# Down-weight pieces loaded earlier, and early down products moved into batch 0's chain, in an attention and feed-forward kernel

## The chip, the cores and the metric

The kernel runs on one core of one Trainium2 chip. The metric is the device time of the whole program in microseconds; the median of several runs is taken. The kernel before takes 239.7 us.

Five engines matter here: TensorE (PE; its weight loads are listed apart as PEld), VectorE (DVE), ScalarE (ACT), GpSimd (POOL), which in this kernel also issues nearly all loads, and SyncE (SP), which issues the stores.

## The reference

Eight batches, eight heads, 576 tokens, head size 64, 32 memory slots. Attention runs through the memory slots, and its output feeds a bilinear feed-forward layer with d_model 512 and d_ff 1536:

```python
a = exp(phi - max) ; a = a / sum(a)             # over the 576 tokens
k_m = einsum('bhsm,bhsd->bhmd', a, k)           # 32 slots per head
v_m = einsum('bhsm,bhsd->bhmd', a, v)
attn = softmax(q @ k_m.T / 8)                   # [576, 32] per head
x = (attn @ v_m) as [4608 tokens, 512]
out = ((x @ w_a) * (x @ w_b)) @ w_out           # f32 out
```

The kernel folds v_m into w_a and w_b, so that x itself is never formed: with A the normalised attention (256 rows, heads x slots), x @ w_a is A times (v_m @ w_a).

## The kernel before

The order of instructions on each engine is the order in which the program emits them. The schedule is written by hand as strings of short names, which call "units". The loads, all on one queue issued by GpSimd, at the start:

```python
load_phi(0); load_q(0, halves); load_v(0)          # batch 0's inputs (k comes by SP and ACT)
...
load_wab(0, 256)                                    # w_a and w_b, first third in two parts
load_wab(256, 512)
...
load_wab(512, 1024)                                 # second third
nc.gpsimd.memset(kv_sbs[1][:, 2], 1.0 / CS)
load_wab(1024, 1536)                                # last third
...
for x in "o0 p o1 k q0 q1 o2 o3 v0 v1 o4 o5".split():
    loads[x]()
```

Here o0 to o5 are the six pieces of w_out (two of its twelve row blocks each), p and k are batch 1's phi and k, and q0, q1, v0, v1 are the halves (heads 0 to 3, heads 4 to 7) of batch 1's q and v. The next inputs, batch 2's and 3's, follow in the same queue.

The units of the attention chain of one batch, as the strings name them:

- exp0, exp1: exp of phi (ACT). ks0, ks1: the sums over tokens for k_m of head groups 0 and 1, and the division (PE product pk, DVE kvm). vs0, vs1: the same for v_m.
- qt0 to qt3: transposes of q on DVE (qT); qt0 and qt1 read the half q0, qt2 and qt3 the half q1. kt, vt: transposes of k_m and v_m on PE (pT), copied by DVE (kvT).
- s0, s1: the scores of head group 0 and 1 (PE, pscore). e0, e1: their exp (ACT, E). den: the sums of exp (PE, pD; then the logarithm on ACT, L). nr: exp(-L) on ACT (R), and the product that gives A.
- hv0, hv1 (256 wide), v1, v2 (512 wide): the fold of v_m into a part of w_a (suffix a) or w_b (suffix b) (PE, pva). hx, x: the copies of that fold out of PSUM, one by ACT and one by DVE (vab).
- a3, b3: the up product of row block 3 with w_a or w_b (pa, pb); a1.0 is one half of the tokens. pa is copied by ACT (a_sb, or w_sums as spare room in batch 0), pb is multiplied with it by DVE (ht).
- F2, f8: fills, products of a constant tile into an unused bank, 512 or 128 columns wide.
- y3: three of the early down products. L: the loads of the batch after the next.

The early down products are the first four blocks of output rows:

```python
EARLY = 4
def early_downs():
    pos = [banks.take([P, d_model], F32, "po", hold=True) for c in range(EARLY)]   # four of eight banks
    for n in range(NFF // 2):              # piece n of w_out
        for c in range(EARLY):
            yield from down_part(*pos[c], c, 2 * n, 2 * (n + 1))                   # two products po
```

That is 48 products, eight for each piece of w_out, and four copies of po by ACT (o_sb) at the end. All of them come after batch 0's last up product in the kernel before. Once all are done a "y" does nothing. Later output rows are made by other products (py, pv, px) that combine sums of the weights (w_sums) and sums of ht (h_sums), both made on GpSimd; "d3" pulls three of those, as far as they are ready.

```python
chain(0, "... a3 b0 hv1b hx1b v1a x1a a2 b3 a4 b2 a5 v1b x1b L a7 a6 b5 v2a x2a b6 b7 a8 v2b a11 x2b b4 a9 a10 b10 b8 b9 b11")
chain(1, "y1 exp0 y6 exp1 y3 ks0 y2 qt0 y1 kt0 y2 qt1 ks1 s0 y1 e0 y2 qt2 kt1 y1 den0 qt3 y6 s1 y3 nr0 e1 y1 vs0 vs1 den1 y2 vt0 vt1 nr1 y3 hv0a hx0a hv0b y3 hx0b")
load(3)
sum_weights()
ups(steps(1, 0, 4), slots(1, "d3+y1+hv1a+hx1a hv1b+y3+hx1b - - - y3+v1+x1a+x1b - -"))
ups(half_steps(1, 0, 4), slots(1, "- v2+x2a+x2b+qt0' - - qt1'+exp0' exp1'+qt2' - kv'+km'+y9"))
```

`ups` emits the up products of a batch and, after each step, one slot of the string beside it; a name with ' is the next batch's unit. kv' and km' are batch 2's sums and their division, kvt its transpose.

Of the kernel before, what the change touches and what calls it, by code (L numbers as in the profile page):

```python
# [14 lines left out]
CS = 16.0  # L15
# [3 lines left out]
def kernel(  # L19
# [11 lines left out]
    nc = tc.nc  # L31
# [6 lines left out]
    NFF = d_ff // P  # L38
    NCH = d_ff // 512
# [19 lines left out]
    wa_rows = moe_w_a.rearrange("(c p) f -> p c f", p=P)  # L59
    wb_rows = moe_w_b.rearrange("(c p) f -> p c f", p=P)  # L60
# [4 lines left out]
    wa_sb = wpool.tile([P, NHP, d_ff], F16, name="wa_sb")  # L65
    wb_sb = wpool.tile([P, NHP, d_ff], F16, name="wb_sb")
    wo_sb = wpool.tile([P, NFF, d_model], F16, name="wo_sb")
    w_sbs = (wa_sb, wb_sb)
# [5 lines left out]
    kv_sbs = [consts.tile([P, 3, NHP, NI * D], F16, name=f"kv_sb{t}") for t in range(2)]  # L74

    def load_phi(b):
        phis[b] = inp.tile([P, NHP, NI * M], F32, name="phi_sb")
        nc.gpsimd.dma_start(out=phis[b], in_=rows(phi, b))

    def load_k(b, hps=slice(0, NHP)):  # L80
        kvs[b] = kv_sbs[b % 2]
        nc.gpsimd.dma_start(out=kvs[b][:, 0, hps], in_=rows(k, b)[:, hps])

    def load_v(b, hps=slice(0, NHP)):
        nc.gpsimd.dma_start(out=kvs[b][:, 1, hps], in_=rows(v, b)[:, hps])

    def load_q(b, hps=slice(0, NHP)):
        if b not in qs:
            qs[b] = inp.tile([P, NHP, NI * D], F16, name="q_sb")
        nc.gpsimd.dma_start(out=qs[b][:, hps], in_=rows(q, b)[:, hps])  # L90

    def load(b):
        load_phi(b)
        load_k(b)
        load_v(b)
        load_q(b)

    def load_wab(lo, hi):
        nc.gpsimd.dma_start(out=wa_sb[:, :, lo:hi], in_=wa_rows[:, :, lo:hi])  # L99
        nc.gpsimd.dma_start(out=wb_sb[:, :, lo:hi], in_=wb_rows[:, :, lo:hi])  # L100

    def load_wo(n):
        sl = slice(2 * n, 2 * (n + 1))
        nc.gpsimd.dma_start(out=wo_sb[:, sl, :], in_=wo_rows[:, sl, :])
# [42 lines left out]
    def fill(n, cols=512):  # L147

        pw = banks.tile([P, 512], F32, name="pw")
        for _ in range(n):  # L150
            nc.tensor.matmul(pw[:, :cols], warm[:, :P], warm[:, :cols], start=True, stop=True)
# [4 lines left out]
    for x in halves:  # L156
        nc.vector.tensor_copy(out=kvs[0][:, 0, x], in_=k_f32[:, x])
    load_wab(0, 256)
    load_wab(256, 512)

    ones = consts.tile([P, 4, 32], F16, name="ones")
# [2 lines left out]
                            pattern=[[-32, 4], [0, 32]], channel_multiplier=1)  # L164
    nc.gpsimd.affine_select(out=ones, in_=ones, compare_op=ALU.is_ge, fill=0.0, base=31,
                            pattern=[[32, 4], [0, 32]], channel_multiplier=-1)
    load_wab(512, 1024)
    nc.gpsimd.memset(kv_sbs[1][:, 2], 1.0 / CS)  # L168
    load_wab(1024, 1536)
    loads = {f"o{n}": lambda n=n: load_wo(n) for n in range(NFF // 2)}  # L170
    loads |= {"p": lambda: load_phi(1), "k": lambda: load_k(1)}
    for n, x in enumerate(halves):
        loads[f"q{n}"] = lambda x=x: load_q(1, x)
        loads[f"v{n}"] = lambda x=x: load_v(1, x)
    for x in "o0 p o1 k q0 q1 o2 o3 v0 v1 o4 o5".split():
        loads[x]()

    attn = {}
# [286 lines left out]
    def sum_weights():  # L465
        nc.gpsimd.tensor_copy(out=w_sums[:, 0, 0, 0:1], in_=attn[1][:, 1, S - 1:S])
        t = [w_sums[:, x] for x in range(4)]
        for out, in0, in1 in ((t[0], quarter(0, 1), quarter(0, 0)), (t[1], quarter(1, 1), t[0]),
                              (t[2], quarter(1, 1), quarter(0, 1)), (t[3], quarter(1, 0), t[1])):
            for x in range(2):  # L470
                sl = slice(KH // 2 * x, KH // 2 * (x + 1))
                nc.gpsimd.tensor_tensor(out=out[:, sl], in0=in0[:, sl], in1=in1[:, sl], op=ALU.subtract)
# [157 lines left out]
    def up_half(b, i, hf, x):  # L630
        ps = banks.tile([P, HALF], F32, name=("pa", "pb")[x])
        for g in range(2):
            nc.tensor.matmul(ps, vabs[b][x][:, g, P * i:P * (i + 1)], attn[b][:, g, HALF * hf:HALF * (hf + 1)],  # L633
                             start=(g == 0), stop=(g == 1))
        if x == 0:
            if b == 0:
                n = (2 * i + hf) % 20
                a_sbs[b, i, hf] = spare[:, HALF * n:HALF * (n + 1)]
            else:
                a_sbs[b, i, hf] = apool.tile([P, HALF], F16, name="a_sb")  # L640
            nc.scalar.copy(out=a_sbs[b, i, hf], in_=ps)  # L641
        else:
            t0 = S * (b % 2) + HALF * hf
            nc.vector.tensor_tensor(out=ht[:, i, t0:t0 + HALF], in0=a_sbs.pop((b, i, hf)), in1=ps, op=ALU.mult)  # L644

    def up(b, i, hfs):
        for hf in hfs:
            up_half(b, i, hf, 0)
        if len(hfs) > 1:
            yield  # L650
        for hf in hfs:
            up_half(b, i, hf, 1)
        yield

    def ups(steps, side=()):

        side = iter(side)
        for step in steps:
            for _ in up(*step):
                work.advance()  # L660
                next(side, us[step[0]]["-"])()
        for f in side:
            work.advance()
            f()

    def steps(b, lo, hi):

        return [(b, i, (0, 1)) for i in range(lo, hi)]

    def half_steps(b, hf, lo=0):  # L670

        return [(b, i, (hf,)) for i in range(lo, NFF)]
# [10 lines left out]
    def slots(b, names):  # L683

        def both(fs):
            return lambda: [f() for f in fs]
        def unit(n):
            if n == "fin":
                return lambda: work.pull(-work.done % NFF)
            if n == "L":  # L690
                return lambda: load(b + 2) if b + 2 < B else None
            if n[0] == "y":
                return lambda: some(int(n[1:]))
            if n[0] == "d" and n[1:].isdigit():
                return lambda: work.pull(int(n[1:]))
            return us[b + n.endswith("'") - n.endswith("_")][n.rstrip("'_")]

        return [both([unit(n) for n in x.split("+")]) for x in names.split()]
# [3 lines left out]
    def some(n):  # L702
        for _ in range(n):
            next(early, None)

    def chain(b, plan):


        for x in plan.split():
            if x[0] in "fF":  # L710
                fill(int(x[1:]), P if x[0] == "f" else 512)
            elif x == "L":
                load(b + 2)
            elif x[0] == "y":
                some(int(x[1:]))
            elif x[0] in "ab":
                i, _, hf = x[1:].partition(".")
                for h in ([int(hf)] if hf else (0, 1)):
                    up_half(b, int(i), h, "ab".index(x[0]))
            else:  # L720
                us[b][x]()

    fill(78, P)
    chain(0, "f2 F1 f8 exp0 ks0 F1 exp1 ks1 qt0 qt1 qt2 F2 kt0 F1 kt1 qt3 s0 e0 s1 e1 F2 f2 den00 den10 vs1 nr00 nr10 vs0 den11 den01 vt0 vt1 nr01 f4 hv0a hx0a F1 nr11 f2 hv0b F1 f2 a1.0 hx0b a0.1 hv1a F1 a1.1 hx1a a0.0 b1 a3 b0 hv1b hx1b v1a x1a a2 b3 a4 b2 a5 v1b x1b L a7 a6 b5 v2a x2a b6 b7 a8 v2b a11 x2b b4 a9 a10 b10 b8 b9 b11")
    chain(1, "y1 exp0 y6 exp1 y3 ks0 y2 qt0 y1 kt0 y2 qt1 ks1 s0 y1 e0 y2 qt2 kt1 y1 den0 qt3 y6 s1 y3 nr0 e1 y1 vs0 vs1 den1 y2 vt0 vt1 nr1 y3 hv0a hx0a hv0b y3 hx0b")
    load(3)
    sum_weights()
    ups(steps(1, 0, 4), slots(1, "d3+y1+hv1a+hx1a hv1b+y3+hx1b - - - y3+v1+x1a+x1b - -"))
    ups(half_steps(1, 0, 4), slots(1, "- v2+x2a+x2b+qt0' - - qt1'+exp0' exp1'+qt2' - kv'+km'+y9"))
    work.plan(S + HALF, 10)  # L730
    ups(half_steps(1, 1, 4), slots(2, "- kvt+qt3 - sc+e0+e1 d1 den0+den1+d1+nr0 - v0+nr1+x0a x0b - v1+x1a+x1b -"))
    second = "v2_+d2+x2a_+x2b_+exp0 - exp1 - kv+km+d2 qt0 d4+qt1+kvt qt2 L+d1+qt3+sc+e0 - d2+v0+e1+x0a+x0b - den0+exp0'+d2 v1+nr0+x1a x1b+d10+exp1' - qt0' v2+x2a+x2b+kv' - den1+km0' km1'+kvd' nr1+qt1' qt2' qt3' - d6"
    every = "exp0' sc+exp1'+e0+d3+e1+v0+x0a+x0b+ed - kv'+km0' km1' - d4+sm0 sm1+tn0+kvd' - tn1+d2 d3 v1+qt0'+x1a+ad d3+L+x1b qt1' - qt2' - v2+x2a+x2b - qt3' - - - - -"
    last = "sc e0+e1+ed - v0+x0b - - sm0 x0a+sm1+tn0 d2+v1+d3+x1b+tn1 - ad+d6 x1a - - - - v2+x2a - - - - - x2b"
# [38 lines left out]
```

The softmax here doesn't subtract the row's maximum and nothing guards it: scores larger than these inputs give would overflow.

## Time and profile before

| what | value |
|---|---|
| time, median of 3 | 239.7 us (239.5 to 240.38) |
| span of the profiled run | 238.1 us |
| PE busy | 229.1 us |
| DVE, POOL, ACT busy | 169.0, 155.0, 153.3 us |
| moved by DMA | 37.27 MB, mean 157 GB/s |

Matmuls are pipelined, so a row of the timeline lasts longer than the time until the next product can start; starts, not ends, are used for spacing. What a row waited for stands at its end in brackets, with the idle time just before it. A transfer's landing is its issue plus the time to landing; how busy a queue is stands in the DMA view.

The timeline of the loads' issue on POOL shows that they are not sent all at once: each waits for an earlier transfer to have landed.

```profile
15.86 0.70 POOL L104 DMA_DIRECT2D wo_sb<-in_moe_w_out_dram  x1 [0.59 <-DMA wa_sb<-in_moe_w_a_dram]
...
24.98 0.71 POOL L90 DMA_DIRECT2D q_sb<-in_q_dram  x1 [1.86 <-DMA wb_sb<-in_moe_w_b_dram]
```

The first column is the start in microseconds, the second the length. The first line is o0, the second q1.

### The profile page before, as it was taken

To read this page: it belongs to the slowest core of one execution; us is meant where nothing else is said; L and a number is where in the kernel's file an instruction comes from. 1 tells how busy PE (TensorE), PEld (TensorE's weight loads), DVE (VectorE), ACT (ScalarE), POOL (GpSimd) and SP (SyncE) were. 2 spreads that over 40 slices of the span, in tenths; PEclk is the share of its full clock that TensorE was granted. 3 is DMA by queue.
4 is the path that set the end of the run, shared out by engine and by line. 5 is a ranking of instruction groups with operands and counts; after the bars stand their busy time and mean duration, and the time that the engine had idled before them with its cause. 6 is when DMAs were issued, how large, how long until landed. Compare 5 with 4: busy or idle time off the path is not lost.

```text
span 238.1 us, 7716 instructions
## 1 busy us (share of the span) xinstructions
PE 229.1 (96%) x3064; PEld 168.5 (71%) x3064; DVE 169.0 (71%) x414; ACT 153.3 (64%) x394; POOL 155.0 (65%) x132
## 2 busy tenths in 40 slices
PE   7979898999999999999999999999999999999993
PEld 7735563455756867867787877867787778888882
DVE  4556874468949968979766888689867776756642
ACT  2267751669699488786878458766876777465430
POOL 7953244599979959592979599682929265946001
PEclk9999999999999999999999999999999999999999
DMA  6999999999975999743799648995233342023145
GB/s 232 240 198 206 216 245 207 249 215 278 226 168 140 207 285 224 160 96 77 173 227 207 108 104 184 221 161 132 58 85 68 72 92 49 21 69 71 38 103 148
DMA packets 38436, 37.27 MB, mean 157 GB/s; under 512 B 14688, under 2 KB 32480, under 8 KB 38400
## 3 DMA queue, kind: packets, MB, share of 16 engines
q0 software_dynamic: 19264, 23.14, 52.4%
q1 hardware_dynamic: 18624, 12.85, 24.2%
q10 hardware_dynamic: 512, 0.79, 1.0%
q8 instruction: 24, 0.39, 0.7%
q14 instruction: 12, 0.10, 0.1%
HBM read 42.47 MB, written 9.44 MB: 218 GB/s over the span
## 4 chain that ended last, share of the span: by engine, by line
PE 77%; DMA 12%; POOL 5%; ACT 2%; issue 1%; DVE 1%; DVEq 0%; POOLq 0%
PE py L505 18%; PE pa L633 17%; PE pb L633 17%; PE pv L505 9%; DMA wa_sb<-in_moe_w_a_dram 6%; DMA wo_sb<-in_moe_w_out_dram 6%; PE pva L368 5%; PE px L505 4%; PE po L429 3%; PE pkv L212 2%; PE pscore L297 1%; POOL wb_sb L100 1%; POOL wa_sb L99 1%; POOL kv_sb L168 1%; ACT a_sb L641 1%
## 5 line engine op out<-in xcount | busy, mean ns | idle before, releaser
L644 DVE TENSOR_TENSOR ht<-a_sb,pb 128x288 f16<-128x288 f16 x168 | 71.8, 445 | 33.5 <-ACT a_sb L641 25.6
L633 PEld LDWEIGHTS <-vab 128*128 128x128 f16 x768 | 72.7, 98 | 24.3 <-issue 7.9
L641 ACT CAST a_sb<-pa 128x288 f16<-128x288 f32 x168 | 65.8, 412 | 31.8 <-PE pa L633 28.6
L633 PE MATMUL pa<-A,vab 128*128 128x288 f16 x384 | 75.9, 287 | 0.0
L633 PE MATMUL pb<-A,vab 128*128 128x288 f16 x384 | 75.3, 286 | 0.2
L487 POOL TENSOR_TENSOR h_sums<-ht 128x768 f16<-128x768 f16 x28 | 46.3, 1656 | 25.8 <-DVE ht L644 25.8
L505 PEld LDWEIGHTS <-h_sums 128*128 128x128 f16 x384 | 37.1, 98 | 8.1 <-issue 1.8
L381 ACT CAST vab<-pva 128x512 f16<-128x512 f32 (+1 forms) x60 | 32.0, 583 | 7.3 <-PE pva L368 7.1
L505 PEld LDWEIGHTS <-ht 128*128 128x128 f16 x288 | 27.9, 98 | 5.9 <-issue 0.9
L505 PE MATMUL py<-w_sums,h_sums 128*128 128x256 f16 x192 | 30.5, 273 | 0.0
L381 DVE CAST vab<-pva 128x512 f16<-128x512 f32 (+1 forms) x44 | 26.6, 635 | 4.4 <-PE pva L368 4.4
L487 POOL TENSOR_TENSOR h_sums<-h_sums,ht 128x768 f16<-128x768 f16 x14 | 23.0, 1644 | 1.0
L487 POOL TENSOR_TENSOR h_sums<-ht,h_sums 128x768 f16<-128x768 f16 x14 | 23.0, 1642 | 0.9
L310 ACT ACTIVATE E<-pscore 128x288 f16<-128x288 f32 x32 | 10.8, 419 | 11.8 <-PE pscore L297 11.7
L505 PE MATMUL py<-w_sums,ht 128*128 128x256 f16 x96 | 16.2, 273 | 0.1
L512 ACT ACTIVATE u<-py 128x256 f32<-128x256 f32 x32 | 12.4, 389 | 5.4 <-PE py L505 4.9
L505 PE MATMUL py<-wo_sb,ht 128*128 128x256 f16 x96 | 15.7, 273 | 0.0
L505 PE MATMUL pv<-w_sums,h_sums 128*128 128x256 f16 x96 | 15.7, 273 | 0.0
L505 PE MATMUL px<-wo_sb,ht 128*128 128x256 f16 x96 | 15.2, 273 | 0.0
L203 DVE STREAM_TRANSPOSE qT<-q_sb 128x288 f32<-128x288 f32 x32 | 14.7, 464 | 0.1
L505 PE MATMUL pv<-wo_sb,h_sums 128*128 128x256 f16 x96 | 14.4, 272 | 0.0
L194 ACT ACTIVATE exp_sb<-phi_sb 128x576 f16<-128x576 f32 x16 | 10.9, 697 | 5.0 <-DMA phi_sb<-in_phi_dram 5.0
(70 smaller groups left out, 267.2 us busy)
## 6 DMA issues: line engine op xcount, KB each, us to landing
out_dram<-o_sb SPq DMA_DIRECT2D x68, 128.0 KB, 2.5
phi_sb<-in_phi_dram POOLq DMA_DIRECT2D x8, 576.0 KB, 7.0
kv_sb<-in_v_dram POOLq DMA_DIRECT2D x7, 576.0 KB, 12.1
kv_sb<-in_k_dram POOLq DMA_DIRECT2D x7, 576.0 KB, 9.7
q_sb<-in_q_dram POOLq DMA_DIRECT2D x6, 576.0 KB, 14.4
wo_sb<-in_moe_w_out_dram POOLq DMA_DIRECT2D x6, 256.0 KB, 12.7
q_sb<-in_q_dram POOLq DMA_DIRECT2D x4, 288.0 KB, 10.9
wa_sb<-in_moe_w_a_dram POOLq DMA_DIRECT2D x2, 512.0 KB, 13.9
```

The source lines that it names most:

```text
L194: nc.scalar.activation(out=t["exp"][:, 2 * z:2 * z + 2, :, :], in_=phis[b][:, 2 * z:2 * z + 2, :].rearrange("p c (i m) -> p c i m", m=M), ...
L203: nc.vector.transpose(out=t["qT"][:, hp, :].bitcast(F32), in_=qs[b][:, hp, :].bitcast(F32))
L310: nc.scalar.activation(out=Ev[:, g, :, z, :], in_=pss, func=AF.Exp, scale=1.0 / (8.0 * CS))
L368: nc.tensor.matmul(t["pva", lo, z][g][0][32 * j:32 * j + 32, 0:hi - lo], t["kvT"][64 * r:64 * r + 64, 4 + g, M * j:M * j + M], w_sbs[z][64 ...
L381: engine_copy(out=vabs[b][z][:, g, lo:hi], in_=pva[:, 0:hi - lo])
L429: nc.tensor.matmul(po, ht[:, i, P * c:P * (c + 1)], wo_sb[:, i, :], start=(i == 0), stop=(i == NFF - 1))
L487: engine.tensor_tensor(out=out, in0=in0, in1=in1, op=op)
L505: nc.tensor.matmul(po, lhs[:, i], rhs[:, i], start=first and i == 0, stop=i == KH - 1, skip_group_check=not first)
L512: nc.scalar.mul(out=x, in_=po, mul=scale)
L633: nc.tensor.matmul(ps, vabs[b][x][:, g, P * i:P * (i + 1)], attn[b][:, g, HALF * hf:HALF * (hf + 1)], start=(g == 0), stop=(g == 1))
L641: nc.scalar.copy(out=a_sbs[b, i, hf], in_=ps)
L644: nc.vector.tensor_tensor(out=ht[:, i, t0:t0 + HALF], in0=a_sbs.pop((b, i, hf)), in1=ps, op=ALU.mult)
```

## The change

The pieces of w_out are spread over the load order: the first goes ahead of the last third of the up weights, the others between batch 1's inputs. With that, eight early down products move into batch 0's chain, ahead of and between the folds of the last third, where PE waited for weights; all 48 are done by the end of batch 1's chain. The fills of batch 0's chain and the order of its units are set anew, and so are the slots after it. The aim is that PE has products to do while it would wait for loads.

```diff
-    load_wab(512, 1024)
-    nc.gpsimd.memset(kv_sbs[1][:, 2], 1.0 / CS)
-    load_wab(1024, 1536)
-    loads = {f"o{n}": lambda n=n: load_wo(n) for n in range(NFF // 2)}
+    loads = {"m": lambda: nc.gpsimd.memset(kv_sbs[1][:, 2], 1.0 / CS)}
+    for n in range(1, NCH):
+        for z in range(2):
+            loads[f"w{'ab'[z]}{n}"] = lambda z=z, n=n: load_w(z, 512 * n, 512 * (n + 1))
...
-    for x in "o0 p o1 k q0 q1 o2 o3 v0 v1 o4 o5".split():
+    for x in "m wa1 wb1 o0 wa2 wb2 p o1 k o2 q0 o3 v0 o4 q1 v1 o5".split():
...
-    chain(0, "f2 F1 f8 exp0 ks0 F1 exp1 ks1 qt0 qt1 qt2 F2 kt0 F1 kt1 qt3 s0 e0 s1 e1 F2 f2 den00 den10 vs1 nr00 nr10 vs0 den11 den01 vt0 vt1 nr01 f4 hv0a hx0a F1 nr11 f2 hv0b F1 f2 a1.0 hx0b a0.1 hv1a F1 a1.1 hx1a a0.0 b1 a3 b0 hv1b hx1b v1a x1a a2 b3 a4 b2 a5 v1b x1b L a7 a6 b5 v2a x2a b6 b7 a8 v2b a11 x2b b4 a9 a10 b10 b8 b9 b11")
-    chain(1, "y1 exp0 y6 exp1 y3 ks0 y2 qt0 y1 kt0 y2 qt1 ks1 s0 y1 e0 y2 qt2 kt1 y1 den0 qt3 y6 s1 y3 nr0 e1 y1 vs0 vs1 den1 y2 vt0 vt1 nr1 y3 hv0a hx0a hv0b y3 hx0b")
+    chain(0, "F1 f2 qt0 F1 exp0 F1 ks0 F1 exp1 ks1 qt1 kt0 qt2 F1 f2 F2 kt1 qt3 F1 s0 e0 s1 F1 e1 F1 den10 f2 den00 f2 vs1 nr00 nr10 vs0 den11 den01 vt0 vt1 nr01 hv0a hx0a nr11 hv0b f4 hx0b a0.0 f2 hv1a F1 a0.1 f2 a1.1 hx1a a1.0 b1 a3 hv1b hx1b v1a b0 x1a a2 b3 a4 v1b x1b a5 b5 y3 b2 L a6 y1 v2a x2a y1 b6 y1 a7 y1 a11 v2b x2b y1 b4 a9 b7 a10 a8 b9 b8 b10 b11")
+    chain(1, "y3 exp0 y5 ks0 y1 exp1 qt0 y5 kt0 qt1 ks1 y1 s0 e0 y2 qt2 y1 kt1 y1 den0 y4 qt3 y3 s1 e1 y1 vs0 vs1 nr0 y1 den1 y5 vt0 vt1 nr1 y3 hv0a hx0a hv0b y1 hx0b y3")
...
-    ups(steps(1, 0, 4), slots(1, "d3+y1+hv1a+hx1a hv1b+y3+hx1b - - - y3+v1+x1a+x1b - -"))
-    ups(half_steps(1, 0, 4), slots(1, "- v2+x2a+x2b+qt0' - - qt1'+exp0' exp1'+qt2' - kv'+km'+y9"))
+    ups(steps(1, 0, 4), slots(1, "d5+y1 hv1a+hx1a hv1b+hx1b - - y3+y3+v1+x1a+x1b - -"))
+    ups(half_steps(1, 0, 4), slots(1, "- v2a+v2b+x2a+x2b - qt0'+exp0' - qt1'+y9 exp1' qt2'+kv'+km'"))
...
-    ups(half_steps(1, 1, 4), slots(2, "- kvt+qt3 - sc+e0+e1 d1 den0+den1+d1+nr0 - v0+nr1+x0a x0b - v1+x1a+x1b -"))
+    ups(half_steps(1, 1, 4), slots(2, "- kvt+qt3 - sc+e0+e1 den0+den1+d1+nr0 - - nr1 v0+x0a+x0b - v1a+v1b+x1a+x1b+d5 -"))
```

`load_w` loads a stretch of w_a or of w_b; `load_wab` calls it for both.

More of the change, by code (lines that the diff above doesn't have):

```diff
@@ L96, in load, with load_w @@
         load_q(b)
+    def load_w(z, lo, hi):
+        nc.gpsimd.dma_start(out=w_sbs[z][:, :, lo:hi], in_=(wa_rows, wb_rows)[z][:, :, lo:hi])
     def load_wab(lo, hi):
-        nc.gpsimd.dma_start(out=wa_sb[:, :, lo:hi], in_=wa_rows[:, :, lo:hi])
-        nc.gpsimd.dma_start(out=wb_sb[:, :, lo:hi], in_=wb_rows[:, :, lo:hi])
+        for z in range(2):
+            load_w(z, lo, hi)
     def load_wo(n):
@@ L166 @@
                             pattern=[[32, 4], [0, 32]], channel_multiplier=-1)
-    load_wab(512, 1024)
-    nc.gpsimd.memset(kv_sbs[1][:, 2], 1.0 / CS)
-    load_wab(1024, 1536)
-    loads = {f"o{n}": lambda n=n: load_wo(n) for n in range(NFF // 2)}
+    loads = {"m": lambda: nc.gpsimd.memset(kv_sbs[1][:, 2], 1.0 / CS)}
+    for n in range(1, NCH):
+        for z in range(2):
+            loads[f"w{'ab'[z]}{n}"] = lambda z=z, n=n: load_w(z, 512 * n, 512 * (n + 1))
+    loads |= {f"o{n}": lambda n=n: load_wo(n) for n in range(NFF // 2)}
     loads |= {"p": lambda: load_phi(1), "k": lambda: load_k(1)}
```

## The prediction

> **What bounds the kernel now.** I read the page's busy shares first, then the table of windows, the PE timeline of the first 65 us, the POOL timeline for the transfers, and the DVE and ACT timelines of the stretch that the change rewrites.
>
> The page: TensorE is busy 96% of the span; no other engine passes 71%.
>
> ```profile
> PE 229.1 (96%) x3064; PEld 168.5 (71%) x3064; DVE 169.0 (71%) x414; ACT 153.3 (64%) x394; POOL 155.0 (65%) x132
> ```
>
> The windows (stretch, its length, busy us of PE, PEld, DVE, ACT, POOL, then clock and DMA) say where the other 4% lies: PE has gaps before 49 us and hardly any from 100 us to 220 us. So a rewritten start can only gain what PE loses there, 1.36 + 1.27 + 0.50 us in these three rows.
>
> ```profile
> 8.00:20.00 12.00, 10.64 (x275) 6.10 (x273) 5.92 (x21) 6.47 (x19) 8.27 (x12) 1.00 1.32 202
> 20.00:37.00 17.00, 15.73 (x159) 9.90 (x161) 12.46 (x29) 11.08 (x30) 5.67 (x9) 1.00 1.22 225
> 37.00:49.00 12.00, 11.50 (x248) 5.05 (x235) 5.58 (x18) 5.24 (x14) 6.74 (x11) 1.00 1.20 230
> ...
> 140.00:180.00 40.00, 39.96 (x514) 30.33 (x513) 30.80 (x76) 29.02 (x75) 27.59 (x20) 1.00 0.76 139
> ```
>
> The PE timeline (start, length, engine, line, operation, tiles, count, idle before) names the four waits on transfers that the change is aimed at, and two rows I use as anchors:
>
> ```profile
> 27.25 0.41 PE L368 MATMUL pva<-wa_sb,kvT 64*32 64x512 f16 x8 [0.20 <-DMA wa_sb<-in_moe_w_a_dram]
> ...
> 29.80 0.41 PE L368 MATMUL pva<-wb_sb,kvT 64*32 64x512 f16 x8 [0.56 <-DMA wb_sb<-in_moe_w_b_dram]
> ...
> 32.11 2.12 PE L633 MATMUL pb<-A,vab 128*128 128x288 f16 x16
> 34.07 2.32 PE L429 MATMUL po<-wo_sb,ht 128*128 128x512 f16 x10
> 36.73 0.69 PE L260 MATMUL pk<-kv_sb,exp_sb 64*32 64x128 f16 x36 [0.34 <-DMA kv_sb<-in_k_dram]
> ...
> 40.75 0.59 PE L429 MATMUL po<-wo_sb,ht 128*128 128x512 f16 x2 [0.50 <-DMA wo_sb<-in_moe_w_out_dram]
> ...
> 43.36 0.45 PE L297 MATMUL pscore<-qT,kvT 32*32 32x288 f16 x16
> ```
>
> These four sum to 1.60 us. PE spacing from the same rows: (34.07 - 32.11)/16 = 0.1225 us for a 288-column product, 0.216 us for a 512-column po (2.32 less the tail of one, 0.376, over nine).
>
> All loads run through one queue whose rate is the limit: for the stretch from 15.9 to 27.5 us, asked alone, the DMA view shows
>
> ```profile
> DMA packets 2802, 2.38 MB, mean 205 GB/s; under 512 B 81, under 2 KB 2800, under 8 KB 2800
> ```
>
> Issue plus time to landing, load by load, gives landings in issue order: second third of wa 22.1, of wb 24.65, last third of wa 27.2, of wb 29.7, o0 31.1, phi 32.5, o1 33.7, k 36.6, q0 38.0, q1 39.5, o2 40.7, o3 42.3, v0 43.4, v1 44.9, o4 46.1, o5 47.5. Here o0 to o5 are the six pieces of the down weight, q0, q1, v0, v1 halves of batch 1's q and v. A piece of wo takes about 1.3 us of the queue, a half of v 1.1 to 1.5, 512 KB of an up weight 2.5.
>
> **What the Trainium skill says.** "TensorE: Matmul & The Clock Gate", Back-to-back issue gap, gives N/2.4 + 2.5 ns for a single gap: 122.5 and 215.8 ns; the two spacings above agree. "DMA: Bandwidth & Descriptors", Queues, rings and completion order, says that descriptors of one ring are consumed in ring order; the landings above come in issue order, so I move landings by moving pieces. "PSUM — Partial Sum Buffer", Specifications, gives eight banks; this kernel's bank list has eight too, and the early down products hold four of them from their first yield on.
>
> **The change, part by part.** Work is conserved: 48 po, the same up products, the same tail. Fills: 98 small and 10 wide before; 94 small and 11 wide after. Only idle moves.
>
> *Front, 8 to 20 us.* Eight small fills before the first pk become two wide ones. The 23 small fills from 4.76 us take 2.46 us with the tail, about 0.1 each: 8 x 0.1 - 2 x 0.22 = 0.36 us earlier. It comes to nothing: the next folds wait for weights at 22.1 and later, and the wait at wb's last third swallows it.
>
> *Weights.* o0 now precedes wa's and wb's last thirds, so they land 1.3 us later: 28.5 and 31.05. Eight po (1.73 us) are put in the way: three after the fold of wb's second third (about 26.4, o0 in at 25.95), five more around the next two folds. PE reaches the wa fold near 27.9 and waits 0.6, reaches the wb fold near 31.0, about when it lands. Then 36 products of 288 columns and one po remain: 31.45 + 36 x 0.1225 + 0.22 = 36.1. Four banks instead of eight under the last sixteen pb let the DVE's 0.41 us per ht hold PE by some 0.3: 36.4. Eight po with o1 (33.7): 38.1, then ks0, k being in since 36.6. Before, ks0 stood at 36.73 with 10 po done; with 16 it would be 38.0. Even.
>
> *Batch 1's chain.* The queue's order is now k o2 q0 o3 v0 o4 q1 v1 o5. The last landing stays 47.5, and only v1 (1.4) and o5 (1.3) follow q1: q1 lands at 47.5 - 2.7 = 44.8 instead of 39.5. The scores of head group 1 (s1) need qt2 and qt3, made from q1. The DVE keeps order qt2, kvT copy, qt3: before, these starts lay 0.4 and 0.2 us apart and a transpose took 0.47, so qt3 is done at 44.87 + 0.44 + 0.21 + 0.46 = 46.0 and s1 starts at 46.05. PE gets there earlier: 38.1 + pk 0.62 + 6 po 1.30 + pT 0.23 + pk 0.62 + po 0.22 + scores 0.37 + 3 po 0.65 + pT 0.23 + po 0.22 + pD 0.24 + 7 po 1.51 = 44.3. It waits 1.7 us. Before, s1 started at 43.36 with 25 po done; after, 34: 43.36 + 9 x 0.216 = 45.30 against 46.05. **Behind by 0.75 us**, although the waits at k, o2 and wb are gone.
>
> *After s1.* All 48 po are now done before batch 1's first up product, and four ScalarE copies of po (1.08 us a pair) fall between R and the first a_sb: PE 46.05 + scores 0.37 + 10 po 2.16 + pk 0.72 + pD, pT, folds 0.71 puts the end of the two 256-wide folds near 50.0 and the 48th po near 50.9; ScalarE does two po copies to 50.7, two vab copies to 51.3, two po copies to 52.35 and only then a_sb. The first ht follows near 52.8. Before it was at 49.79 with 10 po (2.16 us) to come: 51.95. From first ht to the end of batch 2's kv scaling the DVE has 16 ht (5.9), two 256-wide and four 512-wide vab copies (3.2), three transposes (1.2) and the scaling (1.75), 12 us, and its timeline is full from 54 to 63.4:
>
> ```profile
> 54.16 1.29 DVE L381 CAST vab<-pva 128x512 f16<-128x512 f32 x2 [0.52 <-PE pva L368]
> 55.72 1.54 DVE L644 TENSOR_TENSOR ht<-a_sb,pb 128x288 f16<-128x288 f16 x4 [0.27 <-ACT a_sb L641]
> 57.19 1.28 DVE L381 CAST vab<-pva 128x512 f16<-128x512 f32 x2
> ```
>
> So 52.8 + 12.0 = 64.8 instead of 63.44: 1.36 behind, at worst, 0.6 more than at s1. I take half, 0.3, for PE may run ahead by its eight free banks. The denominators of batch 2 move one slot up; ScalarE then does one a_sb copy less before L: -0.3. POOL's sums of the down weight start about 1 us late (nr1 done near 49.7 against 48.7), but its A multiply waited 1.36 us for R, so nothing. Sum: 0.75 + 0.3 - 0.3 = +0.75 us on 239.7: 240.4.
>
> **Rivals.**
> (a) *The intended gain:* q1 comes in time, or PE arrives at s1 later than I say. Then the waits of 1.60 us go, some comes back, and the time is 238.4 to 239.2. For it: after s1 PE had about 1.4 us of slack in the old order up to batch 2's transpose (20.4 us elapsed, 19.0 of products by the spacings above), which a better order can take. Against it: the queue was full without a break, and q1 has 3.7 us more of pieces ahead of it.
> (b) *ScalarE and DVE become the bound* from 49 to 65 us: po copies bunched, no po left to fill PE's waits. All of the 1.36 us stays and the wait shows again at batch 2's transpose: 241.0 to 241.5. For it: DVE full from 54 us. Against it: eight free banks, and batch 2's chain had about a microsecond of slack on PE in 64 to 72 us.
> (c) *Transfers hidden anyway, nothing happens:* 239.5 to 240.0. PE has the same products to do and only a few microseconds of idle in all; what is won at wb, k and o2 (0.56 + 0.34 + 0.50) about equals the new wait at q1.
>
> **Range and chances.** All sizes are below 2 us, under 1% of 239.7, while 2% is 4.8 us: no reading of the idle gives that. Leaning to (c) and (b) over (a), I say 240.4, 8 in 10 between 238.8 and 241.7; faster by over 2% 0.01, within 0.97, slower 0.02.
>
> **What would show it.** Right: in the changed kernel's PE timeline the second group of 16 pscore of batch 1 stands at 46 us with over 1 us idle before it, its DVE transpose waiting on q; no wait at k or o2; the first pva of wb's last third at 31.1; the first batch 1 ht near 52.8. Wrong: q1 landing before 43 us, s1 without a wait, or a first ht before 52 would make (a) true; a po waiting for o5 near 47.5 would show PE ahead of me; and an idle PE beyond 66 us with the DVE busy would show (b).

## The result, and the profile after

| kernel | median | ratio to before, 95% interval |
|---|---|---|
| before | 239.6 us (239.44 to 240.38) | |
| changed | 240.72 us (240.39 to 240.81) | 1.0037 [1.0019, 1.0055] |

The changed kernel is slower by about 0.9 us; the span of the profiled run grew from 238.1 to 238.9 us. The predicted 240.4 us is 0.3 below the median. In short, from what follows: q1 lands late, so the DVE starts batch 1's first ht late, has no free time from there on, and hands the delay to batch 2's scores, which start 0.62 us late. A second chain, early stores that hold up the load of batch 2's q, ends at the same place and hides what an earlier q1 would win.

The page of the changed kernel, its busy shares. PE has three products fewer to do (3061 against 3064, all of them fills), but a row's busy time includes waits within a group; so 230.0 us against 229.1 is no extra work.

```profile
PE 230.0 (96%) x3061; PEld 168.0 (70%) x3061; DVE 168.6 (71%) x414; ACT 152.9 (64%) x394; POOL 154.9 (65%) x132
```

Its table of windows (columns as before):

```profile
20.00:37.00 17.00, 15.97 (x138) 9.31 (x137) 11.47 (x27) 11.19 (x30) 5.68 (x9) 1.00 1.22 224
37.00:49.00 12.00, 11.69 (x237) 5.46 (x235) 4.82 (x16) 3.88 (x10) 6.18 (x9) 1.00 1.20 231
```

PE is busier than before from 20 to 49 us (27.66 against 27.23 us): the filling works. But busy time is not progress. The PE timeline of the changed kernel shows where the won time goes:

```profile
21.99 0.41 PE L372 MATMUL pva<-wa_sb,kvT 64*32 64x512 f16 x8 [0.60 <-DMA wa_sb<-in_moe_w_a_dram]
...
28.36 0.41 PE L372 MATMUL pva<-wa_sb,kvT 64*32 64x512 f16 x8
...
30.98 0.41 PE L372 MATMUL pva<-wb_sb,kvT 64*32 64x512 f16 x8
...
34.22 2.69 PE L637 MATMUL pb<-A,vab 128*128 128x288 f16 x16
36.75 1.89 PE L433 MATMUL po<-wo_sb,ht 128*128 128x512 f16 x8
38.56 0.68 PE L264 MATMUL pk<-kv_sb,exp_sb 64*32 64x128 f16 x36
...
45.47 0.82 PE L301 MATMUL pscore<-qT,kvT 32*32 32x288 f16 x16 [0.22 <-DVE kvT L285]
...
63.95 0.91 PE L245 MATMUL pT<-ident,rep 128*128 128x128 f16 x6
```

The waits at k and o2 are gone, and the two folds at 28.36 and 30.98 show no wait any more. Yet the last sixteen pb now reach the next row after 2.53 us (36.75 - 34.22) instead of 1.96, and s1 at 45.47 takes 0.75 us to its next row, instead of 0.37, as half of it waits for the last transpose. The last row, the transposes of batch 2's k_m and v_m, waits inside too: its next row starts at 64.69 against 64.07 before.

The DVE timeline after:

```profile
44.76 0.48 DVE L207 STREAM_TRANSPOSE qT<-q_sb 128x288 f32<-128x288 f32 x1 [2.73 <-DMA q_sb<-in_q_dram]
...
52.49 0.82 DVE L648 TENSOR_TENSOR ht<-a_sb,pb 128x288 f16<-128x288 f16 x2 [1.46 <-PE pva L372]
...
63.83 0.74 DVE L237 TENSOR_SCALAR rep<-pkv,rphi 128x256 f16<-128x256 f32 x2
```

q1 lands just before 44.76; the first ht of batch 1 stands at 52.49 (before 49.79). From there to the end of batch 2's kv scaling, 64.57, no row names an idle time. Before, that end was 63.44, with 1.9 us of gaps on the way. So 1.13 of the 2.70 us is still missing at the end; the gaps paid the rest. The ScalarE timeline shows one reason for the late first ht, both pairs of copies of po standing ahead of the first a_sb:

```profile
49.54 1.08 ACT L438 ACTIVATE o_sb<-po 128x512 f32<-128x512 f32 x2 [0.32 <-PE po L433]
50.51 0.66 ACT L385 CAST vab<-pva 128x256 f16<-128x256 f32 x2
51.03 1.13 ACT L438 ACTIVATE o_sb<-po 128x512 f32<-128x512 f32 x2
51.99 0.77 ACT L645 CAST a_sb<-pa 128x288 f16<-128x288 f32 x2
```

The prediction left one thing out: finished early, the early output is also stored early. The DMA view of 46 to 60 us (queue, packets, MB, share of the engines; here q0 and q1 are queues, not the halves of q: q0 has the loads, q1 the stores) of the kernel before:

```profile
q0 software_dynamic: 2160, 3.23, 107.8%
q1 hardware_dynamic: 210, 0.36, 7.8%
```

and of the changed one:

```profile
q0 software_dynamic: 1921, 2.86, 95.4%
q1 hardware_dynamic: 547, 0.92, 19.6%
```

The stores took 0.56 MB more in this stretch, the loads got 0.37 MB less. Batch 2's q pays for it. Its line in the DMA view of 41 to 44 us (KB, then us from issue to landing), first before, then changed:

```profile
q_sb<-in_q_dram POOLq DMA_DIRECT2D x1, 576.0 KB, 14.6
```

```profile
q_sb<-in_q_dram POOLq DMA_DIRECT2D x1, 576.0 KB, 17.6
```

It lands at 60.11 us instead of 57.42, just when the DVE, late itself, is done with what comes before; the transpose that reads it stands at 60.15 (before 58.38), with the rest of the DVE's work behind it. The Trainium skill says what I had passed over: "DMA: Bandwidth & Descriptors", Issuing engines are not separate DMA queues, states that transfers begun by different engines run on the same 16 DMA engines and interleave.

**Theories.** (A) q1 late: s1 and all that follows is late by q1's landing. (B) bunched copies: first ht is late for the po copies on ScalarE, and the DVE is then the bound. (C) held banks: four banks gone during the last up products. (D) stores: the early stores hold up batch 2's q. "Lag" below is the start of a row less the start of the same row before.

### The profile page after: what moved, and what is told of

It is laid out like the page before. It is cut to its first block, busy times and chain, and to the rows that moved or that the text cites. A ratio compares the mean times of both kernels' runs of the same rounds, so it can differ in the third digit from the quotient of the medians.

```text
span 238.9 us, 7711 instructions
## 1 busy us (share of the span) xinstructions
PE 230.0 (96%) x3061; PEld 168.0 (70%) x3061; DVE 168.6 (71%) x414; ACT 152.9 (64%) x394; POOL 154.9 (65%) x132
## 4 chain that ended last, share of the span: by engine, by line
PE 75%; DMA 16%; DVE 3%; POOL 2%; issue 1%; ACT 1%; DVEq 0%; POOLq 0%
PE py L509 18%; PE pa L637 17%; PE pb L637 16%; PE pv L509 9%; DMA phi_sb<-in_phi_dram 6%; DMA q_sb<-in_q_dram 5%; PE pva L372 5%; DMA wb_sb<-in_moe_w_b_dram 5%; PE px L509 4%; PE pkv L216 2%; PE po L433 1%; PE pscore L301 1%; DVE ht L648 1%; DVE qT L207 1%; DVE rep L237 1%
## 5 line engine op out<-in xcount | busy, mean ns | idle before, releaser
L637 PE MATMUL pb<-A,vab 128*128 128x288 f16 x384 | 76.2, 287 | 0.3
L509 PE MATMUL px<-wo_sb,ht 128*128 128x256 f16 x96 | 15.2, 273 | 0.0
```

The lines of the kernel that those rows point to most:

```text
L509: nc.tensor.matmul(po, lhs[:, i], rhs[:, i], start=first and i == 0, stop=i == KH - 1, skip_group_check=not first)
```

## The experiments

All stand against the kernel before, timed on the same chip.

| kernel | median us | ratio | 95% interval |
|---|---|---|---|
| changed, again | 240.56 | 1.0037 | [1.0023, 1.0051] |
| load order alone | 243.36 | 1.0143 | [1.012, 1.0166] |
| banks held early, nothing moved | 240.29 | 1.0017 | [1.0004, 1.0031] |
| q1 early | 241.15 | 1.0063 | [1.005, 1.0077] |
| last po later | 241.56 | 1.0077 | [1.0064, 1.0089] |
| q1 early, last po later | 241.12 | 1.0061 | [1.0048, 1.0073] |
| two copies later | 241.01 | 1.0058 | [1.0046, 1.007] |
| one transpose twice | 241.13 | 1.0064 | [1.0051, 1.0077] |
| q1 early, stores later in the program | 241.04 | 1.0059 | [1.0046, 1.0072] |
| q1 early, stores held back | 240.21 | 1.0013 | [0.9993, 1.0033] |
| stores held back, q1 late | 240.79 | 1.0049 | [1.0033, 1.0066] |
| chain 1's inputs first (from before) | 240.86 | 1.0041 | [1.0027, 1.0054] |

**The changed kernel again**, as the reference for the others.

> The changed kernel once more, as the yardstick for the three variants beside it. All theories: ratio to the kernel before 1.003 to 1.005; the second group of scores of batch 1 starts near 45.5 us with its DVE transposes at 44.8 after a wait on q, the first ht of batch 1 near 52.5, the end of batch 2's kv scaling near 64.5.

It came out as the first time, with s1 at 45.27, first ht at 52.29 and the end of kv scaling at 64.66; batch 2's first transpose now shows an idle time of 0.30 us for q. The later rows are compared with this run.

**Load order alone.** The kernel before with the changed kernel's order of loads; no product moved.

```diff
-    for x in "o0 p o1 k q0 q1 o2 o3 v0 v1 o4 o5".split():
+    for x in "m wa1 wb1 o0 wa2 wb2 p o1 k o2 q0 o3 v0 o4 q1 v1 o5".split():
```

> The kernel before with nothing changed but the order of the loads. My theory: the order costs and only the moved products pay for it. Last thirds of the up weights land 1.2 us later (28.3 and 30.9), PE has nothing to do there and waits about 1 us for each; q1 lands at 44.5, so the second group of scores of batch 1 starts near 45.5 instead of 43.36 and PE waits over 1 us for it. Ratio to the kernel before 1.007 to 1.010. Rival (the order does not matter, since the queue's last landing stays at 47.5 and the DVE-bound end from 54 us swallows what comes before): 0.999 to 1.003.

Slower by more than expected. Its PE timeline and its windows (the third number from the end is PE's granted clock):

```profile
45.25 0.82 PE L301 MATMUL pscore<-qT,kvT 32*32 32x288 f16 x16 [1.76 <-DVE kvT L285]
46.00 1.88 PE L433 MATMUL po<-wo_sb,ht 128*128 128x512 f16 x4
```

```profile
45.20:46.00 0.80, 0.67 (x16) 0.23 (x17) 0.72 (x2) 0.00 (x0) 0.59 (x1) 1.00 1.32 279
46.00:48.00 2.00, 2.00 (x26) 0.62 (x24) 0.00 (x0) 0.71 (x2) 0.00 (x0) 0.51 1.07 322
48.00:50.00 2.00, 2.00 (x84) 1.23 (x72) 0.57 (x2) 0.77 (x3) 0.88 (x2) 0.64 1.19 213
```

After a wait of 1.76 us at s1 the granted clock is about half (0.51) for 2 us, and four po are spaced by 0.45 us instead of 0.216. From those po to the transposes of v_m takes 3.85 us (46.00 to 49.85) instead of 2.46: 1.39 us, 0.0058 of the time. Without them the ratio would be near 1.0085, about what was expected. So the new order alone costs about 2 us by its waits and 1.4 more by the clock. The changed kernel, with nine more po done before s1 and the units and fills set anew, has no such wait and wins back most of it, 0.0106 of 0.0143.

**Banks held early.** The kernel before; the four banks of po are taken after b5 in chain 0, as in the changed kernel, and no product moves. The new name h only takes the banks.

```diff
         pos = [banks.take([P, d_model], F32, "po", hold=True) for c in range(EARLY)]
+        yield
...
-    chain(0, "... a7 a6 b5 v2a x2a b6 ...
+    chain(0, "... a7 a6 b5 h v2a x2a b6 ...
```

> The kernel before, with the four PSUM banks of the early down products taken where the changed kernel takes them (after b5 in batch 0's chain), and no product moved. Theory of the four banks: the last sixteen pb of batch 0 take 2.5 us instead of 1.96 and po starts 0.5 us later; the wait for k (0.34) swallows most of it, ratio to the kernel before 1.000 to 1.002. Rival (the sixteen pb were slower in the changed kernel for another reason, such as DVE being behind): 1.96 us again.

```profile
33.22 1.47 PE L634 MATMUL pb<-A,vab 128*128 128x288 f16 x10
34.91 1.13 PE L634 MATMUL pb<-A,vab 128*128 128x288 f16 x6 [0.21 <-DVE ht L645]
35.88 2.32 PE L429 MATMUL po<-wo_sb,ht 128*128 128x512 f16 x10
```

In its PE timeline the po start at 35.88 instead of 34.07, a lag of 1.8 us for an expected 0.5, and the first pk at 38.13 instead of 36.73: PE waits for DVE and ScalarE, which empty the banks (named waits 0.21 us for ht above and 0.24 us for w_sums at 31.45). Chain 1 takes part of it back (s1 lags 0.73 us), and the rest stays: a lag of 0.68 at batch 2's scores, 0.4 us in the time by the ratio and 0.6 by the medians. (C) holds: with nothing else changed, the held banks alone cost about half or more of what the changed kernel lost, and no row named "DMA" shows it.

**q1 early.** The changed kernel with one piece moved.

```diff
-    ... "m wa1 wb1 o0 wa2 wb2 p o1 k o2 q0 o3 v0 o4 q1 v1 o5"
+    ... "m wa1 wb1 o0 wa2 wb2 p o1 k o2 q0 q1 o3 v0 o4 v1 o5"
```

> The changed kernel with q1 loaded before o3 instead of after o4. My theory: the late q1 costs about 0.5 us at the second group of scores (0.22 us of idle ahead of it, and its 16 products last 0.82 instead of 0.45). q1 lands near 40.8, the idle goes, the group starts near 45.2 and lasts 0.45; the program gets 0.3 to 0.5 us shorter than the changed kernel, if the later DVE-bound stretch does not eat it. Rival (only the bunched copies and the full DVE from 52 to 65 us set the time): the group comes earlier, the end does not move, under 0.15 us. Second rival (o3 and o4 now late): a new wait of some tenths at po near 42.3 or 44.8 takes the place of the old one.

s1 lost its wait (45.21, 0.44 us long), first ht came 0.43 us earlier, at 51.86, and the kernel became slower. The DVE timeline shows why:

```profile
60.55 0.48 DVE L207 STREAM_TRANSPOSE qT<-q_sb 128x288 f32<-128x288 f32 x1 [0.95 <-DMA q_sb<-in_q_dram]
...
64.14 0.74 DVE L237 TENSOR_SCALAR rep<-pkv,rphi 128x256 f16<-128x256 f32 x2
```

The DVE arrives sooner and waits 0.95 us for batch 2's q, which lands at 60.52. The scaling ends at 64.88, later than with q1 late. Another 0.5 us was lost at 159 us, where a pkv row waits 0.45 us for v. So (A) alone does not explain the time: with the wait gone, another transfer takes its place.

**Last po later**, with q1 late and with q1 early. Seven po leave chain 1 and fall into the slots after it, so that the copies on ScalarE come later.

```diff
-    chain(1, "... nr1 y3 hv0a hx0a hv0b y1 hx0b y3")
+    chain(1, "... nr1 hv0a hx0a hv0b hx0b")
```

> The changed kernel with the last seven early down products taken out of batch 1's chain, so that they fall into the slots beside the up products, as they did before. My theory: ScalarE's four po copies no longer stand before the first a_sb, PE reaches batch 1's first up product about 1.5 us earlier, the first ht comes near 51 instead of 52.5, batch 2's kv scaling ends 1 us earlier than 64.57, its transposes take 0.5 instead of 0.91, and the program gets 0.3 to 0.7 us shorter than the changed kernel. Rival (PE is the bound there, the order of the same products does not matter): within 0.15 us of the changed kernel.

> Both edits on the changed kernel: q1 before o3, and the last seven early down products in the slots. My theory: the two losses are one after the other, so the gains add, 0.6 to 1.2 us off the changed kernel, ratio to the kernel before 0.998 to 1.001. Rival: both act on the same DVE-bound end, so the two together give no more than the larger one alone.

Both slower than before, and the first clearly slower than the changed kernel. With q1 early too, the first ht is the earliest of all variants of the changed kernel (50.94), and the DVE loses it again, as its timeline shows:

```profile
50.94 0.82 DVE L648 TENSOR_TENSOR ht<-a_sb,pb 128x288 f16<-128x288 f16 x2 [0.87 <-ACT a_sb L645]
...
55.61 1.29 DVE L385 CAST vab<-pva 128x512 f16<-128x512 f32 x2 [1.05 <-PE pva L372]
```

Six po stand in one slot, 1.3 us of PE, and the DVE waits 1.05 us for the fold behind them. Kv scaling ends at 64.95. (B) falls as a remedy, "get the first ht out sooner": the edit moves the products together with their copies, and they then stand where the DVE needs PE. Copies moved alone were not tried.

**Two copies later.** Only the last three po are moved, one after batch 1's fifth step of up products and two after its sixth. The d5 that goes with them found nothing ready there: no tail product stands before 63.13 us in the changed kernel.

```diff
-    chain(1, "... hv0a hx0a hv0b y1 hx0b y3")
+    chain(1, "... hv0a hx0a hv0b y1 hx0b")
...
-    ups(steps(1, 0, 4), slots(1, "d5+y1 hv1a+hx1a hv1b+hx1b - - y3+y3+v1+x1a+x1b - -"))
+    ups(steps(1, 0, 4), slots(1, "- hv1a+hx1a hv1b+hx1b - y1 y2+v1+x1a+x1b - -"))
```

> The changed kernel with its last three early down products moved behind batch 1's second and third up product, so that two of ScalarE's four po copies come after the first a_sb. Theory that the bunched copies hold back the DVE: first a_sb near 51.1 instead of 52.0, first ht near 51.7 instead of 52.5, kv scaling ends 0.5 us earlier, the program 0.3 to 0.5 us shorter than the changed kernel. Rival (the copies only change places, DVE waits for them later instead, or PE loses its filler): within 0.15 us or longer, as when seven products were moved.

```profile
51.94 0.82 DVE L648 TENSOR_TENSOR ht<-a_sb,pb 128x288 f16<-128x288 f16 x2 [0.94 <-PE pb L637]
...
54.80 0.82 DVE L648 TENSOR_TENSOR ht<-a_sb,pb 128x288 f16<-128x288 f16 x2 [0.38 <-ACT a_sb L645]
```

First ht is 0.35 us earlier than in the changed kernel; then the DVE waits further on, 0.38 us of it for an a_sb, and kv scaling ends at 65.02, 0.36 us later than in the changed kernel. Batch 2's q lands at 58.94 here and holds nothing up. Moving the two copies back gains nothing.

**One transpose twice.** The changed kernel with batch 2's first q transpose done a second time: nothing but 0.5 us of DVE work in the stretch that I hold for full. The added unit qt0r repeats qt0.

```diff
-    ups(half_steps(1, 0, 4), slots(1, "- v2a+v2b+x2a+x2b - qt0'+exp0' - ...
+    ups(half_steps(1, 0, 4), slots(1, "- v2a+v2b+x2a+x2b - qt0'+qt0r'+exp0' - ...
```

> The changed kernel with one of batch 2's q transposes done twice, 0.4 us more on DVE between two ht, the result the same. Theory that DVE sets the time from the first ht of batch 1 (52.5) to batch 2's scores: the end of the kv scaling moves from 64.6 to 65.0, the program gets 0.3 to 0.4 us longer than the changed kernel (ratio to the kernel before about 1.005). Rival (PE or a transfer sets it): no change, under 0.1 us.

```profile
60.84 0.48 DVE L416 STREAM_TRANSPOSE qT<-q_sb 128x288 f32<-128x288 f32 x1
...
64.44 0.74 DVE L237 TENSOR_SCALAR rep<-pkv,rphi 128x256 f16<-128x256 f32 x2
```

The scaling ends at 65.18 instead of 64.66, batch 2's scores start at 66.81 instead of 66.30, and the profiled span is 0.57 us longer. All of the added time reaches the end: from batch 2's first transpose on, the DVE's queue sets the time. Just ahead of it, at 60.33, the DVE waited 0.27 us for q.

**q1 early, stores later in the program.** The eight stores are emitted after batch 2's kv sums.

> The kernel with q1 before o3, and besides with the stores of the four early output blocks issued only after batch 2's kv scaling. There the q load of batch 2 landed at 60.5 against 57.4 in the kernel before, and DVE waited 0.95 us for it. Theory that the early stores take the transfer engines from that load: q of batch 2 lands near 57.7, the DVE wait goes, the kv scaling ends near 63.9 instead of 64.9, and the program gets 0.6 to 1.0 us shorter than with q1 early alone, ratio to the kernel before 1.001 to 1.003. Rival (the load is late for another reason, such as its own late issue): q lands at 60 again and nothing changes.

A null experiment: the SP timeline has the stores from 49.63 us on, as with q1 early alone (49.53). Here SP has nothing else to wait for, and the stores went when their o_sb was there, wherever they stand among other engines' instructions. Batch 2's q landed at 60.6.

**q1 early, stores held back.** So SP gets a reason to wait: a transfer of two columns that reads batch 2's scaled rep goes ahead of the stores.

```diff
+        nc.sync.dma_start(out=gate_sb, in_=gates[2][:, 5, 0:2])   # rep of batch 2
         for o_sb, pair, c in late:
             for z in range(2):                                     # the eight stores
```

> q1 before o3, and the eight stores of the early output blocks held back by a tiny transfer ahead of them on the same queue, which reads the result of batch 2's kv scaling. (Emitting the stores later was not enough: they went out at 49.6 us as before.) Theory that the early stores delay batch 2's q load: with none in flight before 64 us, that load lands near 57.7 instead of 60.5, the DVE wait of 0.95 us goes, the kv scaling ends near 63.8, and the program gets 0.5 to 0.9 us shorter than with q1 early alone (ratio to the kernel before 1.002 to 1.004). Rival (the load is late for its own reasons): lands at 60 again, no change.

The stores went from 64.6 us on, and batch 2's q needed 15.4 us instead of 18.1. The DVE timeline, and batch 2's scores in the PE timeline:

```profile
59.52 0.47 DVE L207 STREAM_TRANSPOSE qT<-q_sb 128x288 f32<-128x288 f32 x1
...
63.21 0.74 DVE L237 TENSOR_SCALAR rep<-pkv,rphi 128x256 f16<-128x256 f32 x2
...
65.59 0.77 PE L302 MATMUL pscore<-qT,kvT 32*32 32x288 f16 x32
```

No wait for q; the scaling ends at 63.95, 0.93 us earlier than with q1 early alone, and batch 2's scores start at 65.59 (before 65.58). The time falls by 0.9 us in the medians against q1 early alone, the intervals being apart. (D) is shown, with q1 early. The time is still 0.5 us above the kernel before: 0.28 us of it comes up at batch 3's scores (a row of 0.86 us instead of 0.47; the lag is 0.10 at its start and 0.38 at batch 4's scores) and stays unexplained.

**Stores held back, q1 late**: the fourth corner, the same edit on the changed kernel.

> The changed kernel with q1 late as it is, and only the eight early output stores held back until batch 2's rep has been built, so that they no longer share the transfer engines with batch 2's q load. With it the four combinations of q1 late or early and stores early or late are complete (so far late/early 1.0037, early/early 1.0063, early/late 1.0013). Theory 'two causes in a row': with q1 late the vector engine is 0.5 us later anyway, so that batch 2's q load hardly holds it (the idle before the transpose that reads it is 0.3 us in the changed kernel) and holding back the stores gains at most that: batch 2's q lands at 57.8 instead of 60.3 us, first ht still at 52.4, kv scaling ends at 64.3, ratio 1.002 to 1.003. Rival 'the stores alone': holding them back is worth the 0.005 that it was with q1 early: kv scaling ends near 63.7 and the ratio is 0.998 to 1.000. Rival 'stores cost nothing with q1 late': 1.0035 to 1.004, the q load lands earlier and nothing moves.

The same rows:

```profile
60.12 0.47 DVE L207 STREAM_TRANSPOSE qT<-q_sb 128x288 f32<-128x288 f32 x1
...
63.81 0.74 DVE L237 TENSOR_SCALAR rep<-pkv,rphi 128x256 f16<-128x256 f32 x2
...
66.18 0.77 PE L302 MATMUL pscore<-qT,kvT 32*32 32x288 f16 x32
```

q needs 15.2 us and lands before 58, yet the transpose stands at 60.12 because the DVE is no sooner done with what lies before it: first ht is at 52.46. The scaling ends at 64.55 (expected 64.3), 0.1 us earlier than in the changed kernel, and the time, 1.0049, can't be told from the changed kernel's; the expected 1.002 to 1.003 was missed. Its lag grew by 0.3 us between 158 and 179 us, which I can't explain. The corners side by side:

| ratio | stores early | stores held back |
|---|---|---|
| q1 late | 1.0037 | 1.0049 |
| q1 early | 1.0063 | 1.0013 |

Neither edit alone helps. That both together do is clear by time only against q1 early alone; against the two with q1 late the intervals touch or overlap (1.0023 and 1.0033 are the lower ends there, 1.0033 the upper end here). The traces carry it: the scaling ends at 64.66 and 64.55 with q1 late, 64.88 with q1 early, 63.95 with both. The lag at batch 2's scores says what each is worth when the other is out of the way: with the stores held back, q1 late costs 0.60 us (66.18 against 65.59); with q1 early, the stores cost 0.93 us (66.52 against 65.59). Two chains end at batch 2's transposes, late q1 by the first ht and the stores by the q load, and the later one counts. The banks are held in all four corners: with both edits they leave a lag of 0.01, so whatever they cost there is made up by the waits that went.

**Chain 1's inputs first.** An attempt at a better kernel, from the one before: batch 1's k, q and v ahead of the down weight, the po fitted to it (batch 2's loads and the slots after chain 1 too, not shown).

```diff
-    for x in "o0 p o1 k q0 q1 o2 o3 v0 v1 o4 o5".split():
+    for x in "o0 p k o1 q0 q1 o2 v0 v1 o3 o4 o5".split():
...
-    chain(1, "... exp1 y3 ks0 y2 qt0 ... qt3 y6 s1 y3 nr0 ...
+    chain(1, "... exp1 y1 ks0 y2 qt0 ... qt3 s1 y6 nr0 ...
```

> The kernel before, turned the other way from the change: batch 1's k ahead of o1, its v ahead of o3, batch 2's q ahead of its k, fewer early down products inside batch 1's chain and more beside its up products (16 instead of 11). Theory that po is filler that belongs beside the DVE-bound up products, so that what counts is how early batch 1's first ht comes: no wait at k, first ht near 48.7 instead of 49.79, batch 2's kv scaling ends near 62.5 instead of 63.4, ratio to the kernel before 0.996 to 0.999. Rival (PE alone is the bound, a product done later is a product not done): PE idles inside the chain, ratio 1.000 to 1.004.

```profile
44.96 0.59 PE L432 MATMUL po<-wo_sb,ht 128*128 128x512 f16 x2 [0.42 <-DMA wo_sb<-in_moe_w_out_dram]
```

In the PE timeline the wait at k is gone (ks0 at 35.93, s1 at 40.73) and a po waits for its weights instead. First ht came at 49.24, near the expected 48.7; but sixteen po were still to do beside the up products, the DVE had named gaps of 2.7 us in all, and kv scaling ended at 64.71 instead of the expected 62.5. An early first ht was worth nothing here while PE owed products. No kernel here beats the one before; q1 early with the stores held back can't be told from it.

## Why the prediction was right, point by point

- **The size:** predicted +0.75 us, measured +0.8 in the span and +0.9 to +1.1 in the medians. That the sum agrees is in part luck: its terms were off in both directions, as the points below show.
- **Front:** right that nothing comes of it. It was swallowed sooner than I wrote, by the second third of wa: the fold at 21.99 waits 0.60 us.
- **Weights:** the wb fold at 30.98 (predicted 31.1), no waits at k or o2, as predicted; the expected 0.6 us of waiting at the wa fold (28.36) was hardly there, PE being late itself. The term for four banks was mis-sized: from the wb fold to the po row I had 5.0 us without it and 0.3 for it; it took 5.77, so the banks and small gaps took 0.8. Hence the first pk at 38.56 instead of 38.1, and "even" was a lag of 0.53.
- **Batch 1's chain:** q1 landed at 44.73 (predicted 44.8). But PE reached s1 at 45.25, not 44.3, after the banks and small gaps. The wait of 1.7 us became an idle time of 0.22 and some 0.4 within the row, so my sign of "over 1 us idle" did not show. The lag after s1 was 0.55 at equal products, for a predicted 0.75. The mechanism held: with q1 early the row after s1 stands at 45.59, which is 0.08 us ahead of the kernel before at equal products, so the whole lag is q1's. The banks only used up a lead of 1.0 us (44.3 against 45.30) that the wait for q1 would have taken anyway.
- **After s1:** first ht at 52.49 (predicted 52.8), then 12.08 us of DVE without a gap (predicted 12.0), end of scaling 64.57 (predicted 64.8 at worst). The step that failed is "I take half, 0.3, for PE may run ahead by its eight free banks": 1.13 of the 1.36 us came. Rival (b)'s mechanism was the right one, and the doubled transpose shows it, though (b)'s own sign, an idle PE beyond 66 us, hardly showed (one named wait of 0.20 us up to 70 us). What softened it is that PE lagged by only 0.62 us after batch 2's transposes.
- **The sum itself:** s1's 0.75 and the DVE's 0.3 are not two losses in a row. PE took the lag at s1 back: +0.54 at the first pa, +0.05 at the half steps, -0.19 at batch 2's pkv. Late q1 counts only through the late first ht and the full DVE. So it is one chain, worth +0.62 where it returns to PE, +0.71 at batch 3's scores and +0.75 from there on; with the stores held back, q1 early takes 0.60 of the 0.61 at batch 2's scores away.
- **Denominators, -0.3:** seen, and lost again. ScalarE went from E to L in 1.46 us instead of 1.74. But E followed the start of the scores after 0.73 us instead of 0.49, and the second R lagged by 0.86, so that from batch 2's scores to the second multiply for A it took 5.95 us instead of 5.71. No run isolates it.
- **Not foreseen:** the stores. They cost little with q1 late (held back, batch 2's scores start at 66.18 instead of 66.30), but they are why q1 early, my own explanation turned round, does not bring the time back.

What stays open: the share of the held banks within the changed kernel (the products can't be moved without the banks), and lags of 0.3 to 0.5 us that come up later in single traces.

## What to carry to other kernels

Products moved into a wait only help if what they hold (banks), what they release (copies, stores) and what is put behind them in the load queue has room too; look for each of the three before counting the wait as won. When a removed wait doesn't shorten the time, look for a second chain that ends at the same instruction, and remove both: here each edit alone was worth nothing, and both together brought the work that the two chains end in 0.7 us forward (64.66 to 63.95). And look at what a store that starts earlier does to the loads in flight: here batch 2's q landed 2.6 us later for it (at 60.30 with q1 late, at 57.70 with the stores held back too).

## What was not expected of the hardware

- After a wait of 1.76 us on PE the granted clock went from 1.00 to 0.51 for 2 us and 0.64 for another 2. "TensorE: Matmul & The Clock Gate", What's actually happening, speaks of an idle window of about 3.4 us before the clock falls to a half; this trace shows the half after an idle time of about half that length: PE was busy 1.57 of the 3.41 us up to 46.04, where the clock changes, and 3.40 of the 3.40 us before. A wait of 1.16 us at 28.32 in the same trace left the clock at 1.00. It is one trace, and no run tests what sets the limit.
- Eight stores of 128 KB each made a load of 576 KB that had been issued 7 to 8 us earlier take 18.0 and 18.1 us, where it took 15.2 and 15.4 us with the same stores held back.
- Taking four of eight banks before the fold at 27.41 us instead of after the last up product at 34, with no other edit, delayed the po row by 1.8 us.
